# A fused attention and gated layer: the kv products' last chunk widened to 128 rows with zeros, and all lower parts of the weights made by VectorE

## The chip, the cores and the metric

One core of one Trainium2 chip runs the kernel. The metric is the time of one execution in microseconds of the device; the median of three runs is 863.46 us (861.28 to 864.54). One execution was recorded by the profiler. Engines are named as in the profile: PE is TensorE's matmuls, PEld its weight loads, DVE is VectorE, ACT ScalarE, POOL GpSimd, and SP is SyncE, which issues transfers.

## The reference

An attention without a product of queries and keys, and then a layer with two products and a gate between them.

```python
# q, k, v: (8, 8, 576, 64)
q_s = softmax(q, axis=-1); k_s = softmax(k, axis=2)      # both in the reference with exp(x - max) / (sum + 1e-9)
kv = np.einsum('bhsd,bhse->bhde', k_s, v)                # 64 x 64 for each batch and head
attn = np.einsum('bhsd,bhde->bhse', q_s, kv)
x = attn.transpose(0, 2, 1, 3).reshape(4608, 512)
h = x @ w_in                                             # 512 x 2048
g = h * np.clip(h + 3.0, 0.0, 6.0) / 6.0
out = g @ w_out                                          # 2048 x 512
```

## The kernel before

**Precision.** The weights come as 64-bit numbers, kept as pairs of 32-bit words. `decode(f)` makes fp32 values of them for one of 16 chunks `f` (128 of the 2048 columns of `w_in` and the rows of `w_out` that go with them). Each fp32 operand of a large product is split in two by `split`: ScalarE rounds it to the matmul's format (the high part), and an engine subtracts that from the value (the lower part). A product is then three matmuls: high by high, high by low, low by high.

**The decoding.** `decode(f)` works on 128 x 1024 values: ScalarE's absolute value (L133), VectorE's clamp (L134) and shift with a mask (L136), VectorE's joining of sign and exponent (L141), ScalarE's scaling of the low word (L144), VectorE's addition of it (L145), then the split (L148 to L154): ScalarE's rounding at L120 and the subtraction at L121. The subtraction of the odd chunks from 3 on is given to GpSimd by L153; these are seven: 3, 5, 7, 9, 11, 13 and 15. The others, nine, are VectorE's.

**Attention.** Heads are taken in pairs, four to a batch, so 32 pairs in all. `kv_of` makes the product of a pair's softmaxed keys and its values: 576 rows in four chunks of 128 and a fifth of 64 (`TAIL`), for each of the two heads a 64 x 65 result (the 65th column is the sum of the keys' exponentials, since the values have a column of ones). Each head writes its own half of the 128 partitions of the result `pkv`, so a matmul of a full chunk has the form 128*64 in the profile (rows*columns of the array), and one of the fifth chunk 64*64. The fp32 matmul shows as two matmuls in the trace, so a pair counts 16 and 4. `q_softmax` and `k_softmax` serve batches 0 and 1: there keys come transposed, are turned by TensorE into `pe` and `pe2`, and ScalarE copies them to `ke`, of the fifth chunk only the 64 rows that there are (L246, L247). For the later batches `token_attention` loads keys in five full chunks: the host has filled the last 64 rows of the fifth with the lowest fp32 number, whose exponential is zero, and those of the values with zeros.

**The stages.** Blocks are 512 tokens. Block 0 does attention and both products while the weights are decoded; blocks 1 and 2 do both products (`gemm1`, 12 matmuls of 512 columns into `ph`; the gate, `relu6`; the split of `g` into `gp`; `gemm2`, 12 matmuls into four `po`). The attention of a block is computed during the block before it. During block 1 VectorE also makes sums of weights (`sum_weights`), which are stored and read back. The other 3072 tokens go in three blocks of 1024 through a Strassen-like scheme of seven products instead of eight (`phase1`, `phase2`), whose weight parts are streamed from memory.

**What sets the order.** A scheduler orders the instructions of each engine by a simulation of its own. TensorE's instructions stand in the program's order only from block 1 on; in block 0 the scheduler orders them too. A change of engine for one instruction can therefore move others.

Of the kernel before, what the change touches and what calls it, by code (L numbers as in the profile page):

```python
# [10 lines left out]
F32 = mybir.dt.float32  # L11
# [7 lines left out]
P = 128  # L19
TB = 512  # L20
QD = 32
NC4 = TB // P
# [10 lines left out]
def attention_moe(  # L33
# [15 lines left out]
    nc = tc.nc  # L49

    B, NP, _, S = kT.shape
    D = q.shape[5]
# [7 lines left out]
    NCH = S // P + 1  # L60
    TAIL = S % P
# [14 lines left out]
    def bank_a(name):  # L76
        return ps_a.tile([P, TB], F32, name=name, tag="pa")
# [3 lines left out]
    def ordered(ins):  # L81
        if in_order:
            tc.keep_in_program_order(ins)

    def mm(out, lhsT, rhs, start, stop, goes_on=False):
        ordered(
            nc.tensor.matmul(  # L87
                out, lhsT, rhs, start=start, stop=stop, skip_group_check=goes_on
            )
        )  # L90

    def flip(out, in_):
        ordered(nc.tensor.transpose(out, in_, ident))
# [13 lines left out]
    def place(f, dt, name):  # L107
        return wp.tile([P, 4 * DM], dt, name=name, tag=f"w{f}")
# [7 lines left out]
    FROM_DRAM = 3  # L116
    whole = dr.tile([P, NFC, 2 * DM], F32, name="whole")

    def split(hi, lo, src, engine=nc.vector):
        nc.scalar.copy(hi, src)  # L120
        engine.tensor_sub(lo, src, hi.bitcast(F32))  # L121

    def load_w(f):
        raws[f] = place(f, U32, f"raw_{f}")
# [2 lines left out]
    def decode(f):  # L127

        n = 2 * DM
        pairs = raws.pop(f).rearrange("p (n two) -> p n two", two=2)  # L130
        low, high = pairs[:, :, 0], pairs[:, :, 1]
        m = moe.tile([P, n], F32, name="m", bufs=1)
        nc.scalar.activation(m, high.bitcast(F32), AF.Abs)  # L133
        nc.vector.tensor_scalar(m, m, W_MIN, W_MAX, op0=ALU.max, op1=ALU.min)  # L134
        m = m.bitcast(U32)
        nc.vector.tensor_scalar(  # L136
            m, m, 3, 0x3FFFFFFF, op0=ALU.logical_shift_left, op1=ALU.bitwise_and
        )
        v = moe.tile([P, n], F32, name="v", bufs=3)
        vu = v.bitcast(U32)  # L140
        nc.vector.scalar_tensor_tensor(  # L141
            vu, high, 0xC0000000, m, op0=ALU.bitwise_and, op1=ALU.bitwise_or
        )
        nc.scalar.activation(low, low, AF.Copy, scale=2.0**-29)  # L144
        nc.vector.tensor_tensor(vu, vu, low, op=ALU.add)  # L145
        if f // 2 >= FROM_DRAM:
            nc.sync.dma_start(whole[:, f], v)
        parts = place(f, F32R, f"w_{f}").rearrange("p (s i n) -> p s i n", s=2, i=2)  # L148
        split(
            parts[:, :, 0],  # L150
            parts[:, :, 1],
            v.rearrange("p (s n) -> p s n", s=2),
            nc.gpsimd if f % 2 and f > 1 else nc.vector,  # L153
        )  # L154
        wi[f], wo[f] = parts[:, 0], parts[:, 1]

# [31 lines left out]
    def kv_of(j, hp, ke, vt):  # L188
        pkv = bank_a("pkv")
        for c in range(NCH):  # L190
            r = slice(0, P if c < NC4 else TAIL)
            for h in range(2):
                hs = slice(h * D, (h + 1) * D)
                mm(pkv[hs, 0 : D + 1], ke[r, c, hs], vt[r, c, h, :], c == 0, c == NCH - 1)
        rk = att.tile([P, 1], F32, name="rk", bufs=2)
        nc.vector.tensor_scalar_add(rk, pkv[:, D : D + 1], EPS)
        nc.vector.reciprocal(rk, rk)
        kv = att.tile([P, P], F32, name="kv", bufs=10)
        nc.vector.scalar_tensor_tensor(
            kv.rearrange("p (h d) -> p h d", h=2),  # L200
            pkv[:, 0:D].rearrange("p (o d) -> p o d", o=1).broadcast_to([P, 2, D]),
            rk,
            mask.rearrange("p (h d) -> p h d", h=2),
            op0=ALU.mult,
            op1=ALU.mult,
        )
        kvs[j, hp] = kv
# [29 lines left out]
    def k_softmax(j, km, ke, kt):  # L237
        nc.vector.tensor_reduce(km, kt, axis=AX.X, op=ALU.max, negate=True)
        nc.scalar.activation(kt, kt, AF.Exp, bias=km)
        yield  # L240
        a = bank_a if j else bank
        pe, pe2 = a("pe"), a("pe2")
        for c in range(NC4):
            flip(pe[:, c * P : (c + 1) * P], kt[:, c * P : (c + 1) * P])
        flip(pe2[0:TAIL, 0:P], kt[:, TB:S])
        nc.scalar.copy(ke[:, 0:NC4].rearrange("p c n -> p (c n)"), pe)  # L246
        nc.scalar.copy(ke[0:TAIL, NC4], pe2[0:TAIL, 0:P])  # L247

    def attention(j, hp):

        if not j:
            kt, qt, qT, vt, ke = first[hp]
        else:
            kt, ke, vt = load_k(j, hp)
            qt = att.tile([P, TB], F32, name="qt", bufs=1)
            nc.sync.dma_start(qt, q[j, hp])
            qt = qt.rearrange("p (c h d) -> p c h d", c=NC4, h=2)
        km = att.tile([P, 1], F32, name="km", bufs=2)
        ks = k_softmax(j, km, ke, kt)
        next(ks)  # L260
        q_softmax(qt, j > 0, nc.vector if j else nc.gpsimd)
        yield
        next(ks, None)
        tp = (bank_a if j else bank)("tp")
        for c in range(NC4):
            flip(tp[:, c * P : (c + 1) * P], qt[:, c].rearrange("p h d -> p (h d)"))
        if j:
            qT = att.tile([P, TB], F32, name="qT")
        nc.scalar.copy(qT, tp)
        yield  # L270
        kv_of(j, hp, ke, vt)
        yield
        px = (bank_a if j else bank)("px")
        e = SHIFT * j
        for b, lo, hi in ((j - 1, 0, e), (j, e, TB)):
            if lo < hi:
                mm(px[:, lo:hi], kvs[b, hp], qT[:, lo:hi], True, True)
        x_hi, x_lo = x_block(j)
        split(x_hi[:, hp, :], x_lo[:, hp, :], px)

    def load_k(b, hp, tokens=False):
# [51 lines left out]
    def token_attention(t0, n, hp, put):  # L333
# [28 lines left out]
        for b, (ke, vt, kb) in new.items():  # L362
            kv_of(b, hp, ke, vt)
# [17 lines left out]
    def block_attention(j):  # L381
        def put(c, hp, px):
            x_hi, x_lo = x_block(j)
            split(x_hi[:, hp, :], x_lo[:, hp, :], px)

        return [token_attention(j * TB, TB, hp, put) for hp in range(NP)]
# [328 lines left out]
    for unit in units:  # L715
        next(unit)
        next(unit)
    decode(0)
    for unit in units:
        next(unit, None)  # L720
    decode(1)

    def steps(units, length):
# [32 lines left out]
    for j in range(NB):  # L756
# [10 lines left out]
        for n, f in enumerate(chunks):  # L767
            if not j and f + AHEAD < NFC:
                load_w(f + AHEAD)
            g = gemm1(j, f)  # L770
            if not j and f + 2 < NFC:
                decode(f + 2)
            if j == 1 and f % 2:
                plain_weights(f // 2, 0)
                plain_weights(f // 2, 1)
            if j:
                next(sums, None)
            for _ in range((2 if f % 4 == 3 else 1) if not j else 2 if n < 14 else 1):
                next(step, None)
            if j == NB - 1 and n == 8:  # L780
                fetch(2)
            if j == NB - 1 and n >= 14:
                for _ in range(3):
                    next(fac, None)
            pend.append((j, n, f, g))
            while len(pend) > (LAG if not j else 1):
                work(*pend.pop(0))
# [91 lines left out]
```

## Time and profile before

| what | value |
|---|---|
| median of three runs | 863.46 us (861.28 to 864.54) |
| the profiled execution, its own time | 863.42 us |
| its span from the first instruction to the last | 861.6 us |
| TensorE busy | 816.8 us (95%) |
| VectorE busy | 683.7 us (79%) |
| ScalarE busy | 443.6 us (51%) |
| GpSimd busy | 80.1 us (9%) |

The busy share of an engine is a mean over stages. In block 0, the first 146 us, VectorE is nearly always at work; later TensorE is. A row of the timeline gives start, length (both in us), engine, line, operation, output and inputs, shapes, the count of merged instructions, and in brackets how long the engine was idle before and what ended that. A row of a group gives busy time and mean length. A row of the waits gives the total in us, the times, and the longest. An instruction on VectorE is shown somewhat longer than the time after which the next one starts.

### The profile page before, as it was taken

How to read it: one execution, taken by the hardware profiler on the slowest of the kernel's cores; microseconds unless marked ns; L12 is line 12 of the kernel's file. 1: busy time of each engine (PE TensorE's matmuls, PEld its weight loads, DVE VectorE, ACT ScalarE, POOL GpSimd, SP SyncE). 2: the span in 40 equal slices, each digit the busy share in tenths (PEclk: the TensorE clock that was granted, in tenths of full speed). 3: DMA queues.
4: the chain of work that ended last, by engine and by line, in shares of the span. 5: the costliest groups of instructions: out<-in, count | busy, mean ns of one | idle time of the engine just before them, and what ended most of it. 6: DMA issues, size and time to landing. Idle time of an engine off the chain costs nothing.

```text
span 861.6 us, 11761 instructions
## 1 busy us (share of the span) xinstructions
PE 816.8 (95%) x4032; PEld 654.0 (76%) x4032; DVE 683.7 (79%) x1088; ACT 443.6 (51%) x717; POOL 80.1 (9%) x178
## 2 busy tenths in 40 slices
PE   4689998999999998999999999999999999999997
PEld 3468786877887876887877777777788788887886
DVE  7998998998778988578998985688597845648763
ACT  7886673443344444345555553544555534445543
POOL 5111212110100110001102000011000000000000
PEclk9789999999999999999999999999999999999999
DMA  9997667578549660578875667775566776666672
GB/s 366 413 407 265 210 201 233 198 243 279 169 150 366 213 240 25 169 259 272 271 256 167 194 205 238 225 229 168 172 178 193 236 231 195 193 193 191 193 234 88
DMA packets 75643, 192.30 MB, mean 223 GB/s; under 512 B 7232, under 2 KB 19520, under 8 KB 73536
## 3 DMA queue, kind: packets, MB, share of 16 engines
q1 hardware_dynamic: 75008, 190.51, 67.3%
q10 hardware_dynamic: 576, 1.05, 0.3%
q8 instruction: 32, 0.52, 0.2%
q14 instruction: 27, 0.22, 0.1%
HBM read 147.49 MB, written 44.04 MB: 222 GB/s over the span
## 4 chain that ended last, share of the span: by engine, by line
PE 67%; DVE 18%; DMA 5%; issue 4%; ACT 3%; POOL 1%; SPq 0%; ACTq 0%; DVEq 0%; POOLq 0%
PE x L87 24%; PE po L87 12%; PE ph L87 10%; PE y L87 9%; PE z L87 9%; DMA kt<-in_kT_dram 2%; DVE g L515 2%; PE px L87 2%; PE pkv L87 2%; DVE gp L121 1%; DVE gf L121 1%; DVE v L141 1%; DVE right L121 1%; DVE km L347 1%; DMA wf<-gp 1%
## 5 line engine op out<-in xcount | busy, mean ns | idle before, releaser
L120 ACT CAST gf<-g 128x512 fp32r<-128x512 f32 x168 | 103.9, 622 | 96.3 <-DVE gf L121 48.0
L87 PE MATMUL ph<-x,w 128*128 128x512 f32 x576 | 147.9, 405 | 4.4 <-POOL w L121 2.0
L87 PE MATMUL po<-w,gp 128*128 128x512 f32 x576 | 146.9, 404 | 3.5 <-DVE gp L121 2.2
L121 DVE TENSOR_TENSOR gf<-g,gf 128x512 fp32r<-128x512 f32 x168 | 112.9, 686 | 31.8 <-ACT gf L120 31.0
L87 PEld LDWEIGHTS ph<-x,w 128*128 128x128 f32 x576 | 111.7, 195 | 31.5 <-POOL w L121 2.9
L87 PEld LDWEIGHTS po<-w,gp 128*128 128x128 f32 x576 | 108.4, 192 | 29.4 <-DVE gp L121 3.3
L87 PE MATMUL x<-right,gp 128*128 128x512 f32 x384 | 95.0, 392 | 2.9 <-DVE g L555 2.9
L87 PE MATMUL x<-gf,gp 128*128 128x512 f32 x384 | 89.0, 389 | 0.0
L87 PEld LDWEIGHTS x<-right,gp 128*128 128x128 f32 x384 | 71.6, 188 | 19.2 <-DVE g L555 3.7
L87 PEld LDWEIGHTS x<-gf,gp 128*128 128x128 f32 x384 | 72.1, 188 | 15.0
L514 ACT ACTIVATE g<-ph,three 128x512 f32<-128x512 f32 x48 | 32.8, 686 | 64.6 <-PE ph L87 64.6
L120 ACT CAST gp<-g 128x512 fp32r<-128x512 f32 x48 | 29.6, 620 | 39.8 <-DVE g L515 39.7
L514 ACT ACTIVATE v<-g,three 128x1024 f32<-128x1024 f32 x24 | 27.6, 1151 | 42.4 <-DVE g L559 42.4
L87 PE MATMUL x<-right,left 128*128 128x512 f32 x192 | 47.8, 392 | 0.8 <-DVE g L555 0.8
L87 PE MATMUL y<-right,gp 128*128 128x512 f32 x192 | 48.2, 395 | 0.0
L87 PE MATMUL x<-gf,left 128*128 128x512 f32 x192 | 46.1, 392 | 0.9 <-DVE gf L121 0.9
L87 PE MATMUL z<-gf,gp 128*128 128x512 f32 x192 | 45.7, 392 | 1.0 <-DVE gf L121 0.9
L87 PEld LDWEIGHTS z<-gf,gp 128*128 128x128 f32 x192 | 35.7, 188 | 10.1 <-DVE gf L121 2.7
L87 PEld LDWEIGHTS x<-gf,left 128*128 128x128 f32 x192 | 35.7, 188 | 10.1 <-DVE gf L121 2.8
L87 PEld LDWEIGHTS x<-right,left 128*128 128x128 f32 x192 | 35.7, 188 | 8.6 <-DVE g L555 1.3
L87 PEld LDWEIGHTS y<-right,gp 128*128 128x128 f32 x192 | 35.6, 188 | 8.0 <-issue 0.5
L514 ACT ACTIVATE g<-g,three 128x512 f32<-128x512 f32 x24 | 17.4, 725 | 39.5 <-DVE g L548 39.5
(135 smaller groups left out, 1324.6 us busy)
## 6 DMA issues: line engine op xcount, KB each, us to landing
gp<-wf SPq DMA_DIRECT2D x112, 512.0 KB, 3.6
left<-wf SPq DMA_DIRECT2D x56, 512.0 KB, 3.7
raw<-in_w_dram SPq DMA_DIRECT2D x16, 1024.0 KB, 14.2
wf<-gp SPq DMA_DIRECT2D x64, 256.0 KB, 3.6
wf<-w SPq DMA_DIRECT2D x48, 256.0 KB, 3.9
vt<-in_v_dram SPq DMA_DIRECT2D x28, 325.0 KB, 5.4
kt<-in_kT_dram SPq DMA_DIRECT2D x28, 288.0 KB, 3.5
ke<-in_k_dram SPq DMA_DIRECT2D x24, 320.0 KB, 4.7
```

The source lines that it names most:

```text
L87: nc.tensor.matmul(out, lhsT, rhs, start=start, stop=stop, skip_group_check=goes_on)
L120: nc.scalar.copy(hi, src)
L121: engine.tensor_sub(lo, src, hi.bitcast(F32))
L141: nc.vector.scalar_tensor_tensor(vu, high, 0xC0000000, m, op0=ALU.bitwise_and, op1=ALU.bitwise_or)
L347: nc.vector.tensor_reduce(km, kt, axis=AX.X, op=ALU.max)
L514: nc.scalar.activation(r, h, AF.Relu, bias=three, scale=1.0)
L515: nc.vector.scalar_tensor_tensor(g, r, 6.0, h, op0=ALU.min, op1=ALU.mult)
```

## The change

Two edits. `kv_of` takes all 128 rows of every chunk, the fifth included, so that all its matmuls have the form 128*64. Where batches 0 and 1 fill `ke` from the turned keys, GpSimd now writes zeros to the 64 rows that were left unwritten: eight memsets of 64 x 128. And `split` has no choice of engine any more: all sixteen lower parts of the weights are subtracted by VectorE.

```diff
-    def split(hi, lo, src, engine=nc.vector):
+    def split(hi, lo, src):
         nc.scalar.copy(hi, src)
-        engine.tensor_sub(lo, src, hi.bitcast(F32))
+        nc.vector.tensor_sub(lo, src, hi.bitcast(F32))
...
             v.rearrange("p (s n) -> p s n", s=2),
-            nc.gpsimd if f % 2 and f > 1 else nc.vector,
         )
...
         for c in range(NCH):
-            r = slice(0, P if c < NC4 else TAIL)
             for h in range(2):
                 hs = slice(h * D, (h + 1) * D)
-                mm(pkv[hs, 0 : D + 1], ke[r, c, hs], vt[r, c, h, :], c == 0, c == NCH - 1)
+                mm(pkv[hs, 0 : D + 1], ke[:, c, hs], vt[:, c, h, :], c == 0, c == NCH - 1)
...
         nc.scalar.copy(ke[0:TAIL, NC4], pe2[0:TAIL, 0:P])
+        nc.gpsimd.memset(ke[TAIL:P, NC4], 0.0)
```

Lines behind the edits move up: by one from L154 on, by two from L191 on, and by one again from L248 on. The scheduler's order changes in blocks 0 and 1; behind these it is the same but for a few places.

At the end of block 0, VectorE's order before. `v_1160` is the last chunk's decoded weights (chunk 15, made at L145), `x1_564` is block 1's input, `g_1255` and `gp_1258` are the first gated product of block 1 and its lower part; the subtraction for chunk 15 is not among these rows, since it is GpSimd's.

```order
L145 ISA v_1160<-raw_15_942,v_1160 128x2048
L347 TENSOR_REDUCE km_1287<-kt_1281 128x1
L433 TENSOR_TENSOR v_1264<-v_1261 128x256
L435 TENSOR_TENSOR v_1264<-v_1261 128x256
L196 TENSOR_SCALAR rk_986<-pkv_975 128x1
L121 TENSOR_TENSOR gp_1153<-g_1150,gp_1153 128x512
L312 TENSOR_REDUCE qm_1291<-qt_1279 128x16
L434 TENSOR_TENSOR v_1264<-v_1264,v_1261 128x256
```

The same place after the change: `v_1168` is chunk 15's weights, `w_15_1173` their parts.

```order
L145 ISA v_1168<-raw_15_950,v_1168 128x2048
L346 TENSOR_REDUCE km_1707<-kt_1696 128x1
L432 TENSOR_TENSOR v_1272<-v_1269 128x256
L434 TENSOR_TENSOR v_1272<-v_1269 128x256
L197 SCALAR_TENSOR_TENSOR kv_997<-pkv_983,rk_994,mask_80 128x128
L304 TENSOR_TENSOR qm_1299<-qm_1299,swap_1302 128x16
L514 SCALAR_TENSOR_TENSOR g_1201<-g_1201,ph_1188 128x512
L121 TENSOR_TENSOR gp_1161<-g_1158,gp_1161 128x512
L433 TENSOR_TENSOR v_1272<-v_1272,v_1269 128x256
L121 TENSOR_TENSOR w_15_1173<-v_1168,w_15_1173 128x2x512
```

The last subtraction of the weights now stands on VectorE, nine instructions behind the last decoded chunk. Counted from the start, 198 instructions stand up to and with block 1's first lower part of g before, and 205 now.

GpSimd's order before, from its last instruction for the first attention to the first for block 2; `w_3` to `w_15` are the seven lower parts.

```order
L235 TENSOR_TENSOR kq3_109<-kq3_109,qr_166 128x512
L121 TENSOR_TENSOR w_3_422<-v_418,w_3_422 128x2x512
L121 TENSOR_TENSOR w_5_534<-v_530,w_5_534 128x2x512
L121 TENSOR_TENSOR w_7_686<-v_681,w_7_686 128x2x512
L121 TENSOR_TENSOR w_9_821<-v_816,w_9_821 128x2x512
L121 TENSOR_TENSOR w_11_972<-v_967,w_11_972 128x2x512
L121 TENSOR_TENSOR w_13_1074<-v_1069,w_13_1074 128x2x512
L349 COPY kb_1289<-km_1287 128x128
L121 TENSOR_TENSOR w_15_1165<-v_1160,w_15_1165 128x2x512
```

The same stretch now:

```order
L233 TENSOR_TENSOR kq3_109<-kq3_109,qr_166 128x512
L246 MEMSET ke_544 64x128
L246 MEMSET ke_697 64x128
L246 MEMSET ke_849 64x128
L348 COPY kb_1297<-km_1295 128x128
```

The subtractions are gone and three memsets for batch 1's keys stand in their place; the other five stand among the constants at the program's start.

TensorE's order at the start of block 0, before: `ph_339`, `ph_395` and `ph_443` are the first products of chunks 0 to 2, `pkv_473` the kv product of batch 1's first pair, `po_489` the first of the four second products.

```order
L87 MATMUL ph_339<-x0_311,w_0_306 128x512 x2
L87 MATMUL ph_395<-x0_311,w_1_334 128x512 x2
L93 MATMUL pe_425<-ident_75,kt_369 128x128 x4
L93 MATMUL pe2_426<-ident_75,kt_369 64x128
L87 MATMUL ph_443<-x0_311,w_2_366 128x512 x6
L93 MATMUL tp_434<-ident_75,qt_374 128x128 x4
L87 MATMUL pkv_473<-vt_372,ke_371 64x65 x10
L87 MATMUL po_489<-w_0_306,gp_355 128x512 x2
```

And now, with `ph_343`, `ph_399`, `ph_448` and `po_494` in the same parts:

```order
L87 MATMUL ph_343<-x0_315,w_0_310 128x512 x2
L87 MATMUL ph_399<-x0_315,w_1_338 128x512 x2
L87 MATMUL ph_448<-x0_315,w_2_370 128x512 x12
L93 MATMUL pe_429<-ident_75,kt_373 128x128 x4
L93 MATMUL pe2_430<-ident_75,kt_373 64x128
L87 MATMUL po_494<-w_0_310,gp_359 128x512 x2
```

The second products of chunk 0 now stand ahead of the turned queries and the kv product of batch 1's first pair, and behind all of chunk 2's first product.

## The prediction

> **What bounds the kernel now.** I read the page's busy shares first, then one table of busy time by stage, then TensorE's waits in block 0, then single instructions around GpSimd's subtractions and around the kv products. The stages are the start, the rest of block 0 (weights decoded while the first tokens are multiplied), the part that holds the later attention, and the rest.
>
> ```profile
> PE 816.8 (95%) x4032; PEld 654.0 (76%) x4032; DVE 683.7 (79%) x1088; ACT 443.6 (51%) x717; POOL 80.1 (9%) x178
> ...
> 0.00:40.00 40.00, 20.47 (x141) 14.59 (x142) 34.30 (x59) 31.13 (x46) 11.49 (x20) 0.87 0.97 388
> 40.00:146.00 106.00, 98.84 (x487) 78.07 (x487) 99.81 (x135) 72.87 (x147) 21.50 (x17) 0.95 0.76 272
> 146.00:620.00 474.00, 463.32 (x2381) 369.39 (x2382) 384.92 (x655) 224.25 (x346) 47.07 (x142) 0.99 0.66 213
> 620.00:861.60 241.60, 234.15 (x1027) 191.92 (x1025) 164.71 (x241) 115.34 (x180) 0.00 (x0) 1.00 0.64 194
> ```
>
> The columns behind the length of a stage are TensorE, its weight loads, VectorE, ScalarE, GpSimd, then TensorE's granted clock. From 146 us on TensorE is busy 98% of the time (463.32 of 474.00, 234.15 of 241.60) and VectorE 81% and 68%: what TensorE does there is paid in full. From 40 to 146 us it is the other way round in rank: VectorE 99.81 of 106 us (94%), TensorE 98.84 at a clock of 0.95. Both are nearly full, and who waits for whom decides.
>
> ```profile
> PE ph L87 <- POOL w L121: 2.0, 2, 1.3
> PE ph L87 <- DVE x L121: 1.3, 1, 1.3
> ...
> 105.98 4.13 PE L87 MATMUL ph<-x,w 128*128 128x512 f32 x10 [1.30 <-POOL w L121]
> ...
> 138.05 4.61 PE L87 MATMUL ph<-x,w 128*128 128x512 f32 x19 [0.72 <-POOL w L121]
> ...
> 145.89 0.74 PE L87 MATMUL ph<-x,w 128*128 128x512 f32 x2 [1.31 <-DVE x L121]
> 146.47 3.89 PE L87 MATMUL po<-w,gp 128*128 128x512 f32 x10
> ```
>
> TensorE's late waits in block 0 are for lower weight parts made by GpSimd (2.0 us) and for VectorE's lower part of x (1.3 us). So block 0 ends when VectorE and GpSimd have delivered.
>
> **The lower parts of the weights.** Seven subtractions leave GpSimd and join VectorE. What one costs there, and what it costs today:
>
> ```profile
> L121 POOL TENSOR_TENSOR w<-v,w x7: 2357/2642/2991, 39.8 to 135.2; 128x1024 fp32r<-128x1024 f32 x7
> ...
> 97.30 1.22 DVE L121 TENSOR_TENSOR w<-v,w 128x1024 fp32r<-128x1024 f32 x1
> 98.43 1.22 DVE L141 SCALAR_TENSOR_TENSOR v<-raw,m 128x1024 uint32<-128x1024 uint32 x1
> ...
> L141 DVE SCALAR_TENSOR_TENSOR v<-raw,m x15: 1210/1218/3249, 23.2 to 129.6; 128x1024 uint32<-128x1024 uint32 x15
> L136 DVE TENSOR_SCALAR m<-m x15: 679/693/2936, 22.4 to 127.8; 128x1024 uint32<-128x1024 uint32 x15
> L145 DVE CUSTOM_DVE_ANT_0 v<-raw,v x15: 1210/1216/3109, 24.6 to 132.5; 128x2048 uint16<-128x2048 uint16 x15
> ...
> 39.83 2.94 DVE L136 TENSOR_SCALAR m<-m 128x1024 uint32<-128x1024 uint32 x1
> 54.67 2.64 POOL L121 TENSOR_TENSOR w<-v,w 128x1024 fp32r<-128x1024 f32 x1 [12.46 <-ACT w L120]
> 55.14 3.25 DVE L141 SCALAR_TENSOR_TENSOR v<-raw,m 128x1024 uint32<-128x1024 uint32 x1
> 71.59 2.85 DVE L145 CUSTOM_DVE_ANT_0 v<-raw,v 128x2048 uint16<-128x2048 uint16 x1
> 91.29 3.25 DVE L141 SCALAR_TENSOR_TENSOR v<-raw,m 128x1024 uint32<-128x1024 uint32 x1
> 103.75 2.72 DVE L136 TENSOR_SCALAR m<-m 128x1024 uint32<-128x1024 uint32 x1
> 122.41 3.11 DVE L145 CUSTOM_DVE_ANT_0 v<-raw,v 128x2048 uint16<-128x2048 uint16 x1
> 134.65 0.41 DVE L435 TENSOR_TENSOR v<-v 128x256 f32<-128x256 f32 x1
> 136.71 1.57 DVE L434 TENSOR_TENSOR v<-v 128x256 f32<-128x256 f32 x1
> ```
>
> On VectorE a subtraction takes 98.43 - 97.30 = 1.13 us from its start to the next start: seven are 7.9 us more work on a nearly full engine. Against that stand seven long VectorE instructions, one inside or at the edge of each GpSimd subtraction. The one at 55.14 shows why: GpSimd's started at 54.67 and ended at 57.31, and VectorE's ended at 58.39, 1.08 us later, about its own usual length. It stood until GpSimd was through. Over the medians (L136 0.69, L141 1.22, L145 1.22; the 0.41 of L435 for L434, of the same shape) the seven lose 2.25 + 2.03 + 1.63 + 2.03 + 2.03 + 1.89 + 1.16 = 13.0 us. So the move takes 13.0 us off VectorE and puts 7.9 us on: 5.1 us less. The same rows in the order shown say that ahead of the first lower part of g in block 1 stand exactly seven more instructions than before, the subtractions, and nothing else. I take -5.1 us for the end of block 0. Bounds: at the least the 2.0 us that TensorE waits for GpSimd go; at the most TensorE's whole idle time of that stage, 106.00 - 98.84 = 7.2 us. The balance lies between, and VectorE is the engine that is late, so I keep it.
>
> The Trainium skill speaks on both sides of this. Its page "Perfetto Trace Analysis", section "Optimizing Scalar/DVE Operations", says that with a saturated VectorE handing work even to GpSimd may make sense, though between these two it might not help, as they share a read port; its page "SBUF — State Buffer", section "Who interferes with whom", says the loser of that port blocks for a whole instruction. By the first half of the former rule alone the change would cost its 7.9 us; by the latter the blocks go too. The row at 55.14 agrees with the latter.
>
> The scheduler orders block 0 anew. The first second-layer product now stands right behind the third first-layer product instead of behind the kv products too, and on SyncE two of the last raw loads stand ahead of stores of weight parts that they stood behind. Neither puts a thing that VectorE waits for further back, and VectorE's own order decides; I cost the new order at nothing, with VectorE's backlog as its cover. If that cover is gone, TensorE's idle time is what is left to win or lose.
>
> **The kv products.** One head pair now is 20 matmuls of one form instead of 16 and 4:
>
> ```profile
> 161.94 0.69 PE L87 MATMUL pkv<-vt,ke 128*64 128x65 f32 x16
> ...
> 162.10 0.40 PE L87 MATMUL pkv<-vt,ke 128*64 128x65 f32 x8
> ...
> 162.55 0.33 PE L87 MATMUL pkv<-vt,ke 64*64 64x65 f32 x4
> 162.82 0.50 PE L87 MATMUL po<-w,gp 128*128 128x512 f32 x1
> ...
> 259.24 1.83 PE L87 MATMUL pkv<-vt,ke 128*64 128x65 f32 x40
> 261.00 0.50 PE L87 MATMUL po<-w,gp 128*128 128x512 f32 x1
> ...
> 426.94 1.83 PE L87 MATMUL pkv<-vt,ke 128*64 128x65 f32 x40
> ...
> 599.30 0.95 PE L87 MATMUL pkv<-vt,ke 128*64 128x65 f32 x20
> ...
> L87 PE MATMUL pkv<-vt,ke 128*64 128x65 f32 x384 | 16.5, 228 | 0.0
> L87 PE MATMUL pkv<-vt,ke 64*64 64x65 f32 x96 | 8.0, 243 | 0.0
> ```
>
> A single group takes 162.82 - 161.94 = 0.88 us. Its 16 matmuls of the form 128*64 hold TensorE until the four of 64*64 start at 162.55: 0.61 us. Those four hold it 0.27 us. The second row is a view of the single moment 162.30: eight matmuls are under way, each 222 ns long, so one starts every 28 ns. Four more in the same run would take 0.11 us instead of 0.27: 0.16 us saved. A double group takes 261.00 - 259.24 = 1.76 us and changes form three times inside; as one run it would be 0.61 + 24 x 0.028 = 1.28 us, 0.48 saved. From 146 us to 620 there are 96/4 = 24 such groups: eight singles (first at 161.94, last at 599.30) and eight doubles (first at 259.24, last at 426.94): 8 x 0.16 + 8 x 0.48 = 5.1 us. By the last two rows, averages by form (16.5/384 = 43 ns, 8.0/96 = 83 ns), it would be 96 x 40 ns = 3.9 us. I take the middle, 4.5 us, and keep both as ends. All of it lies where TensorE is 98% busy. The eight groups ahead of 146 us save as much each, but VectorE covers them: nothing.
>
> The Trainium skill's page "TensorEngine Tiling (Array Packing)", section "Key Properties", says that a change of tiling mode drains the engine, which these rows bear out (0.27 us for four matmuls). Its section "Theoretical Speedup" speaks against the change: a contraction of 64 rows or fewer may go up to twice as fast when tiled.
>
> The zeros are eight memsets of 64 x 128 on GpSimd, two at most for one buffer's turn. The nearest row:
>
> ```profile
> 1.44 0.14 POOL L99 MEMSET mask<- 64x64 f32 x1
> ```
>
> Twice that size I call 0.2 us, 1.6 us in all, on an engine that is 9% busy, beside ScalarE's copy into the same buffer. What stands behind the last of them on GpSimd, copies of maxima for block 2's keys, is wanted only for block 2's kv products. Free; a late one would show as a kv product that waits for GpSimd.
>
> **The sum.** The profiled execution took 863.42 us (its span 861.6), next to the median 863.46. 863.4 - 5.1 - 4.5 = 853.8, rounded 854.
>
> **The rivals.** *VectorE pays and gets nothing back.* If the long instructions are long for another cause, the 7.9 us come on top of a full stage: 863.4 + 7.9 - 4.5 = 866.8, slower. For it: VectorE is at 94%. Against it: all seven fall on GpSimd's seven, and none of the fifteen medians shows it elsewhere. It decides once less than 3.4 of the 13.0 us come back. By the skill's rule of handing work to GpSimd this is the case to fear. Chance 0.04.
> *The new order starves TensorE in block 0.* Stage 40 to 146 has a clock of 0.95, so idle time there is paid again in clock (5% of 106 is 5.3 us). If the front of block 0 waits as much more as VectorE wins, only the kv term is left: 863.4 - 4.5 = 858.9, and anything up to 861. Chance 0.16.
> *The form change costs nothing by itself* and four more full matmuls replace four half ones at the same price, the case in which tiled small products are as quick as the tiling page's table hopes: 863.4 - 5.1 = 858.3. Against it: 83 ns against 43. Chance 0.07.
> *Block 1 takes the lead back.* VectorE there waits for transfers of weights that must be written and read again:
>
> ```profile
> 189.66 4.43 DMA v<-whole
> ...
> 195.61 2.86 DMA wf<-gp
> ```
>
> Both lie on the chain that ended last. If they come no earlier, the gain of block 0 stops at TensorE's slack there, and about half of 5.1 is left: 863.4 - 2.5 - 4.5 = 856.4. Chance 0.15.
>
> **How the numbers follow.** Both terms in full, 851 to 856: 0.58. The range runs from both at their best, 863.4 - 7.2 - 5.1 = 851.1, and a little below since the clock of block 0 may rise too (849.5), up to the starved case's 860.5. A measurement here tells about 0.5% (4.3 us) from no change, so faster means under 859.1: the forecast 0.58, the last two rivals 0.22, near none of the first, and a third of the starved case's 0.16 make some 0.82; I say 0.81. Slower, over 867.8, needs the first rival and more: 0.04. The rest, 0.15, is no change.
>
> **What would show it.** The first lower part of g in block 1 stands here now:
>
> ```profile
> 149.89 0.69 DVE L121 TENSOR_TENSOR gp<-g,gp 128x512 fp32r<-128x512 f32 x1 [0.69 <-ACT gp L120]
> ```
>
> Right: no VectorE row of L136, L141 or L145 over 2 us from 40 us on; TensorE's wait for GpSimd gone; this row some 5 us earlier; single kv groups near 0.72 us and doubles near 1.28, all 128*64. Wrong: VectorE's busy time from 40 to 146 us no lower in sum, new waits of TensorE for g or x in block 0, a clock below 0.95 there, or kv groups still at 0.88.

## The result, and the profile after

The changed kernel takes 852.38 us (median of six runs, 848.81 to 856.43), the kernel before beside it 862.26: a ratio of 0.9885, 95% interval 0.9854 to 0.9915. Run again in another session it took 850.45 us against 861.5, ratio 0.9856 (0.9831 to 0.988). So the change saves 10 to 11 us. The profiled execution took 852.34 us, its span 850.6.

The page's busy shares and the first three of the four stages of before (columns as there):

```profile
PE 807.8 (95%) x4032; PEld 646.5 (76%) x4032; DVE 677.9 (80%) x1095; ACT 442.6 (52%) x717; POOL 66.1 (8%) x179
...
0.00:40.00 40.00, 24.90 (x168) 18.43 (x169) 34.31 (x59) 31.93 (x46) 12.84 (x25) 0.96 0.97 390
40.00:146.00 106.00, 98.54 (x490) 75.86 (x489) 100.15 (x151) 74.75 (x152) 5.37 (x13) 0.98 0.80 283
146.00:620.00 474.00, 460.24 (x2396) 368.33 (x2395) 388.03 (x658) 226.72 (x348) 47.88 (x142) 1.00 0.64 215
```

VectorE is as full between 40 and 146 us as it was (100.15 us, before 99.81), but in that time it now does 151 instructions, before 135. Seven more instructions in the whole program, and 5.8 us less busy time (677.9, before 683.7).

The three operations that had long instances, as VectorE's groups with the shortest, median and longest length, then the first lower part of g in block 1 (the second of the two merged here, at 142.78 us):

```profile
L141 DVE SCALAR_TENSOR_TENSOR v<-raw,m x15: 1208/1219/1301, 23.1 to 124.8; 128x1024 uint32<-128x1024 uint32 x15
L136 DVE TENSOR_SCALAR m<-m x15: 678/685/695, 22.4 to 122.3; 128x1024 uint32<-128x1024 uint32 x15
L145 DVE CUSTOM_DVE_ANT_0 v<-raw,v x15: 1204/1216/1226, 24.4 to 129.1; 128x2048 uint16<-128x2048 uint16 x15
...
142.21 1.25 DVE L121 TENSOR_TENSOR gp<-g,gp 128x512 fp32r<-128x512 f32 x2
```

No instance is above 1.30 us, and block 1's first lower part stands at 142.78, 7.1 us earlier than the 149.89 of before.

TensorE's waits from 35 to 146 us (total, times, longest), all of them:

```profile
PE ph L87 <- ACT w L120: 2.6, 2, 2.3
PE po L87 <- ACT gp L120: 2.2, 3, 1.6
PE tp L93 <- DVE qt L233: 1.1, 2, 0.6
PE pe L93 <- ACT kt L237: 0.6, 1, 0.6
PE po L87 <- DVE gp L121: 0.3, 1, 0.3
PE ph L87 <- DVE w L121: 0.3, 1, 0.3
```

The wait for GpSimd's lower parts is gone, and so is that for x. TensorE now waits here mostly for ScalarE. In sum it waits as long as before in this stretch (7.1 us, before 7.2), but the stretch now holds more of its work.

The kv products, from TensorE's timeline: a single group and the product behind it, then a double one, then the two that answer to the rows at 426.94 and 599.30 of before, and the group over the whole program.

```profile
153.70 0.80 PE L87 MATMUL pkv<-vt,ke 128*64 128x65 f32 x20
154.44 0.50 PE L87 MATMUL po<-w,gp 128*128 128x512 f32 x1
...
250.44 1.39 PE L87 MATMUL pkv<-vt,ke 128*64 128x65 f32 x40
251.75 0.50 PE L87 MATMUL po<-w,gp 128*128 128x512 f32 x1
...
414.79 1.39 PE L87 MATMUL pkv<-vt,ke 128*64 128x65 f32 x40
588.50 0.80 PE L87 MATMUL pkv<-vt,ke 128*64 128x65 f32 x20
...
L87 PE MATMUL pkv<-vt,ke 128*64 128x65 f32 x560 | 20.7, 225 | 0.0
```

A single group holds TensorE for 0.74 us (before 0.88), a double one for 1.31 (before 1.76). The same four groups serve as milestones of TensorE, since they stand at the same places of the work. Ahead of them the table has the product `po` that the kernel before starts at 146.47, just behind the last wait of block 0. Each column is headed by the start in the kernel before, and the rows tell how many us earlier (negative) or later each kernel is there, in its one profile:

| kernel, its profiled span | 146.47 | 161.94 | 259.24 | 426.94 | 599.30 | 861.6 (end) |
|---|---|---|---|---|---|---|
| changed, 850.6 | -7.2 | -8.2 | -8.8 | -12.2 | -10.8 | -11.0 |
| changed, other session, 850.0 | -7.2 | -8.2 | -8.5 | -10.9 | -11.3 | -11.6 |
| weights edit alone, 856.8 | -6.3 | -7.9 | -2.9 | -4.7 | -4.7 | -4.8 |
| weights edit with the memsets, 863.3 | -3.0 | -4.6 | +1.1 | +2.0 | +1.8 | +1.7 |
| kv edit alone, 857.5 | -0.3 | -1.9 | -1.3 | -3.6 | -4.1 | -4.1 |
| GpSimd writes zeros, 852.4 | -6.9 | -8.5 | -7.9 | -10.0 | -10.3 | -9.2 |
| changed, with useless multiplications, 857.5 | +0.3 | -0.7 | -0.3 | -3.5 | -3.9 | -4.1 |

The last five rows are experiments told below. From the first column to the second four of the kernels gain 1.6 us and the other three 1.0. That is not their doing: right behind 146 us the kernel before, in its profiled execution, ran at a granted clock of 0.72. The stretch in it, and the answering one of the changed kernel:

```profile
146.00:152.00 6.00, 6.00 (x20) 4.78 (x21) 4.70 (x8) 2.70 (x5) 0.00 (x0) 0.72 0.40 131
...
139.00:145.00 6.00, 5.67 (x25) 4.38 (x24) 5.83 (x12) 4.32 (x8) 0.00 (x0) 1.00 0.20 57
```

So 7 of the 11 us are there when block 0 ends, 1 comes right behind it by this clock, and about 3 come later. Whether other executions of the kernel before slow down there too is not shown; the kernel with the fifth chunk in the middle, told below, has the same order of instructions and ran that place at 1.00.

### The profile page after: what moved, and what is told of

Read it like the earlier page. It is cut to its first block, busy times and chain, and to the rows that moved or that the text cites. A ratio compares the mean times of both kernels' runs of the same rounds, so it can differ in the third digit from the quotient of the medians.

```text
span 850.6 us, 11778 instructions
## 1 busy us (share of the span) xinstructions
PE 807.8 (95%) x4032; PEld 646.5 (76%) x4032; DVE 677.9 (80%) x1095; ACT 442.6 (52%) x717; POOL 66.1 (8%) x179
## 4 chain that ended last, share of the span: by engine, by line
PE 63%; DVE 21%; DMA 5%; ACT 4%; issue 4%; POOL 2%; SPq 0%; ACTq 0%; DVEq 0%; POOLq 0%
PE x L87 26%; PE y L87 10%; PE z L87 9%; PE po L87 8%; PE ph L87 8%; DVE gp L121 2%; DVE g L514 2%; DMA qt<-in_qf_dram 2%; PE px L87 2%; POOL swap L303 2%; DVE v L141 1%; DMA kt<-in_kT_dram 1%; DVE v L145 1%; ACT qt L219 1%; PE pkv L87 1%
## 5 line engine op out<-in xcount | busy, mean ns | idle before, releaser
L87 PE MATMUL ph<-x,w 128*128 128x512 f32 x576 | 143.8, 397 | 2.9 <-ACT w L120 2.6
L87 PEld LDWEIGHTS po<-w,gp 128*128 128x128 f32 x576 | 106.0, 189 | 33.9 <-ACT gp L120 5.9
L87 PEld LDWEIGHTS ph<-x,w 128*128 128x128 f32 x576 | 108.6, 190 | 28.4 <-ACT w L120 3.3
```

Of the source, the lines that this page charges most:

```text
L87: nc.tensor.matmul(out, lhsT, rhs, start=start, stop=stop, skip_group_check=goes_on)
```

## The experiments

**Each edit alone.** First the kernel before with the lower parts on VectorE, the kv products as they were:

```diff
-    def split(hi, lo, src, engine=nc.vector):
+    def split(hi, lo, src):
...
-        engine.tensor_sub(lo, src, hi.bitcast(F32))
+        nc.vector.tensor_sub(lo, src, hi.bitcast(F32))
...
-            nc.gpsimd if f % 2 and f > 1 else nc.vector,
```

> The kernel before with all lower parts of the weights on VectorE, the kv products as they were. Theory (GpSimd's subtractions held VectorE up, 13.0 us against 7.9 us of added work): 5 to 8 us faster, about 855 to 857 us, no L136, L141 or L145 over 2 us after 40 us, kv groups still 0.88 us. Rival (the gain of the change is the kv products', and the end of block 0 came earlier by the new order's luck): within 2 us of before.

Measured: 863.79 us against 862.07, ratio 1.0012 (0.9996 to 1.0029): nothing. Its twelve runs are not of one kind: two took 857.77 and 858.62 us, ten 862.59 to 865.47, and the profile is of the 858.62. Then the kernel before with the kv products on 128 rows and the zeros, the weights as they were:

```diff
-            r = slice(0, P if c < NC4 else TAIL)
...
-                mm(pkv[hs, 0 : D + 1], ke[r, c, hs], vt[r, c, h, :], c == 0, c == NCH - 1)
+                mm(pkv[hs, 0 : D + 1], ke[:, c, hs], vt[:, c, h, :], c == 0, c == NCH - 1)
...
+        nc.gpsimd.memset(ke[TAIL:P, NC4], 0.0)
```

> The kernel before with the kv products on 128 rows alone, GpSimd's seven subtractions kept. Theory: 24 groups behind 146 us save 0.147 us (single) or 0.442 us (double), 4.7 us in all, of which the changed kernel kept about 3: 3 to 5 us faster, 857 to 859 us, the seven long VectorE instructions still there. Rival (all of the gain is block 0's): within 1 us of before.

Measured: 857.72 us, ratio 0.9956 (0.9941 to 0.9971), so 2.5 to 5.1 us saved. Apart 0 and 4 us, together 10 to 11: the parts do not add up. The table above says where. With the weights edit alone, in the profile of the faster kind, TensorE is 7.9 us ahead at the first milestone, and 5.0 us of it are lost by the second. The largest loss is at the largest wait of TensorE in block 1, here with VectorE's rows ahead of it (the weights edit alone):

```profile
196.03 0.68 DVE L121 TENSOR_TENSOR x<-px,x 128x512 fp32r<-128x512 f32 x1
196.63 0.74 DVE L346 TENSOR_REDUCE km<-kt 128x1 f32<-128x576 f32 x1
...
198.23 0.68 DVE L311 TENSOR_REDUCE qm<-qt 128x16 f32<-128x512 f32 x1
...
209.08 0.70 DVE L321 STREAM_TRANSPOSE m<-qt 128x512 f32<-128x512 f32 x1
...
209.84 1.14 PE L87 MATMUL px<-m,kv 128*128 128x128 f32 x4 [4.02 <-DVE m L321]
```

And the same instructions in the changed kernel:

```profile
194.06 0.68 DVE L311 TENSOR_REDUCE qm<-qt 128x16 f32<-128x512 f32 x1
...
196.31 0.68 DVE L121 TENSOR_TENSOR x<-px,x 128x512 fp32r<-128x512 f32 x1
196.91 0.74 DVE L346 TENSOR_REDUCE km<-kt 128x1 f32<-128x576 f32 x1
...
204.80 0.70 DVE L321 STREAM_TRANSPOSE m<-qt 128x512 f32<-128x512 f32 x1
...
205.56 1.14 PE L87 MATMUL px<-m,kv 128*128 128x128 f32 x4 [1.10 <-DVE m L321]
```

Both kernels are at the same place at 196 us (`x<-px` and `km` stand 0.3 us apart). But the queries' maximum, L311, stands ahead of them in VectorE's queue in the changed kernel and behind them with the weights edit alone. From it to TensorE's `px` it is a chain of small steps of 11.5 us in the one (205.56 - 194.06) and 11.6 in the other. So L311 4.2 us later makes `px` 4.3 us later. That is the work of the scheduler: the kv edit, which touches neither instruction, changes its order. Over this `px` the lead on the kernel before falls from 7.3 to 4.5 us (it stands at 214.35 there, behind a wait of 1.22), and to 3.0 over the matmuls right behind it, with a granted clock of 0.89 from 200 to 215 us.

**Is it the zeros or the kv products that change the order?** The weights edit with the eight memsets, the kv products still on 64 rows.

> The first experiment's kernel (all subtractions on VectorE, fifth chunk of 64 rows) with the eight memsets added, which nothing reads; the order on TensorE and VectorE is that of the first experiment. Theory (the split's gain reaches the end of block 0 and is lost again behind it, in a wait that differs from run to run): the end of block 0 some 8 us earlier than before, then a loss in block 1 or 2; 858 to 865 us, and the profile may show the 6 us that the first profile did not. Rival (the first experiment was slow for want of the zeros, or the memsets cost time): another time than 858 or 864 us.

Measured: 864.25 us against 861.5, ratio 1.0032 (1.001 to 1.0053). The order is that of the weights edit alone, and the wait is there too (L322 here is L321 there). From TensorE's timeline and from the busy time between 215 and 290 us (granted clock third from the end), of this kernel:

```profile
213.86 1.83 PE L87 MATMUL px<-m,kv 128*128 128x128 f32 x4 [4.62 <-DVE m L322]
...
215.00:290.00 75.00, 73.11 (x375) 59.22 (x374) 54.84 (x101) 30.46 (x48) 6.40 (x28) 0.96 0.60 205
```

and of the weights edit alone in its fast profile:

```profile
215.00:290.00 75.00, 73.11 (x389) 59.73 (x388) 58.55 (x110) 31.68 (x50) 6.92 (x30) 1.00 0.62 216
```

With the same busy time of TensorE, 375 matmuls against 389 get done, at a clock of 0.96 against 1.00. So the zeros alone do not help, and the slower of these two profiles loses work to the clock behind such a wait. It does so elsewhere too: of the 6.5 us between the two spans 3.3 are there at the first column of the table already. From 50 to 55 us the granted clock was 0.66 in the slower one and 1.00 in the faster, from 103 to 109 us 0.72 and 1.00. The kernels differ by the memsets alone, and TensorE, VectorE and ScalarE have the same order in both. There is no profile of one of the ten slower runs of the weights edit alone; that they lose their time in the same way is likely, not shown, and why two of twelve escape stays open.

**Does a change of form cost, or the number of matmuls?** The kernel before with the fifth chunk in the middle of the group, so that one more change of form lies inside it and nothing else is different:

```diff
-        for c in range(NCH):
+        for n, c in enumerate((0, 1, NC4, 2, 3)):
...
-                mm(..., c == 0, c == NCH - 1)
+                mm(..., n == 0, n == NCH - 1)
```

> The kernel before with the fifth chunk of the kv products in the middle (chunks 0, 1, 4, 2, 3): the same matmuls in the same forms, but one more change of form in each group. Theory (the change of form is what costs): a single group some 0.1 us longer, 0.96 to 1.00 us instead of 0.88, the whole 2 to 4 us slower. Rival (the 64-row matmuls are slow in themselves): groups still 0.88 us and the time the same.

Measured: 863.29 us, ratio 1.0016 (1.0004 to 1.0027), so 0.3 to 2.3 us. The answering single group, from TensorE's timeline of this kernel:

```profile
162.05 1.10 PE L87 MATMUL pkv<-vt,ke 128*64 128x65 f32 x20
163.07 1.21 PE L87 MATMUL po<-w,gp 128*128 128x512 f32 x4
```

It takes 163.07 - 162.05 = 1.02 us where it took 0.88: 0.147 more by the exact starts, in the double groups too. The change takes one such step out of a single group (0.879 to 0.732) and three out of a double one (1.758 to 1.316): 0.147 each, to the last digit. Sixteen groups behind 146 us make 2.4 us; the whole is slower by 1.2 by the medians. The group is longer than the 0.96 to 1.00 us that were expected and the whole less slow than the 2 to 4 us, but the rival's 0.88 us is out. So a change of form costs 0.147 us, and four matmuls on 64 rows are no cheaper than four on 128. The Trainium skill's page "TensorEngine Tiling (Array Packing)", section "Key Properties", says that a change of tiling mode drains TensorE. These groups agree, at 0.147 us a change. The two-fold gain of its section "Theoretical Speedup" does not show. No matmul here used the other 64 rows at the same time; that this is why is argued, not shown.

**Is it GpSimd's reading that holds VectorE up?** The kernel before, with GpSimd writing zeros to its seven lower parts; the kv products unchanged:

```diff
+        if engine is nc.gpsimd:
+            nc.gpsimd.memset(lo.bitcast(F32), 0.0)
+        else:
+            engine.tensor_sub(lo, src, hi.bitcast(F32))
```

> The kernel before, but the seven lower parts that were GpSimd's are filled with zeros by it instead of subtracted: GpSimd writes as much, and reads nothing. (These lower parts are left out of the computation.) Theory A (what holds VectorE up is GpSimd's reading through a shared port): L141, L145 and the others at their usual length, 5 us or more faster. Theory B (any GpSimd work on SBUF holds VectorE up for as long as it lasts): VectorE instructions longer by the memset's length wherever they meet.

Measured: 854.2 us, ratio 0.9906 (0.989 to 0.9921): 7.9 us saved, with TensorE's form changes all still there. VectorE does not get the seven subtractions here, and its order differs from before in some 50 places. In block 1 the queries' maximum stands ahead of `x<-px` and `km`, as in the kernel before and the changed one, and the lead lasts there (-8.5, then -7.9). Lines are three further down in this kernel (L144 is the joining L141, L137 the clamp L134). A group, the memsets, and two of them with what VectorE did beside them:

```profile
L144 DVE SCALAR_TENSOR_TENSOR v<-raw,m x15: 1212/1218/1226, 23.1 to 123.4; 128x1024 uint32<-128x1024 uint32 x15
...
L122 POOL MEMSET w<- 128x1024 f32 x7 | 6.7, 956 | 88.0 <-DVE v L148 73.2 <-DMA vt<-in_v_dram 13.6 <-issue 1.2
...
50.48 0.95 POOL L122 MEMSET w<- 128x1024 f32 x1 [10.93 <-DVE v L148]
50.97 0.67 DVE L124 TENSOR_TENSOR gp<-g,gp 128x512 fp32r<-128x512 f32 x1
...
113.23 0.95 POOL L122 MEMSET w<- 128x1024 f32 x1 [14.03 <-DVE v L148]
113.30 1.42 DVE L137 TENSOR_SCALAR m<-m 128x1024 f32<-128x1024 f32 x1
```

A subtraction with two inputs ran at its usual length beside a memset (50.97 to 51.64, the memset to 51.43). The clamp, with one input and usually 0.69 us, did not: at 113.30 it took 1.42, and ended 0.54 us behind the memset. Four more clamps were stretched so, all 2.2 us together against 13.0 before. So for instructions with two inputs, 8.7 of the 13.0 us, it is the reading, as far as this run goes: no joining and no addition met a memset. For those with one, L136 with 4.3 us before and the clamp here, writing is enough; how much of their smaller loss comes from a memset's 0.95 us in place of 2.64 is not told apart. The Trainium skill's page "SBUF — State Buffer", section "Who interferes with whom", says both: that two inputs contend only with a GpSimd that reads, and that a tensor_scalar in a two-port mode contends in any case. Both agree, if the clamp is such a one (0.69 us, where a subtraction of this shape takes 1.13).

Then the other way round: the changed kernel, in which GpSimd multiplies each of the same seven chunks by one, in place, with the orders of TensorE and VectorE unchanged:

```diff
+        if f % 2 and f > 1:
+            nc.gpsimd.tensor_mul(v, v, ones.broadcast_to([P, n]))
```

> The changed kernel with seven extra GpSimd multiplications by one, in place on the same seven chunks' values: no engine's result needs them, and TensorE's and VectorE's orders stay as they are. Theory (GpSimd's reading holds VectorE up): the seven VectorE instructions of 2.5 to 3.3 us come back, VectorE is busy 10 to 14 us more ahead of 146 us, the end of block 0 comes 7 to 13 us later, 860 to 865 us. Rival (the gain came from where the subtractions stand and from their shorter latency, not from the hold-up): within 2 us of the changed kernel's 852.4.

Measured: 858.42 us against 862.47, ratio 0.9952 (0.9937 to 0.9967): 6 to 7 us of the gain are gone, which the rival cannot explain. The time is below the expected 860 to 865 us, since less of the hold-up came back: four VectorE instructions took 2.7 to 2.9 us and two more were stretched in part, 8.5 us in all instead of 10 to 14. Lines are two further down here (L143 the joining, L147 the addition). These two groups, the useless multiplications, one of them with VectorE's row in it, and block 1's first lower part (the second of two):

```profile
L143 DVE SCALAR_TENSOR_TENSOR v<-raw,m x15: 1206/1221/2915, 23.7 to 132.2; 128x1024 uint32<-128x1024 uint32 x15
L147 DVE CUSTOM_DVE_ANT_0 v<-raw,v x15: 1208/1217/2799, 25.1 to 136.5; 128x2048 uint16<-128x2048 uint16 x15
L157 POOL TENSOR_TENSOR v<-v,ones 128x1024 f32<-128x1024 f32 x7 | 20.6, 2940 | 79.3 <-DVE w L123 36.6 <-DMA whole<-v 16.8 <-DVE rk L198 13.6
...
92.89 2.24 POOL L157 TENSOR_TENSOR v<-v,ones 128x1024 f32<-128x1024 f32 x1 [4.46 <-DMA whole<-v]
93.41 2.80 DVE L147 CUSTOM_DVE_ANT_0 v<-raw,v 128x2048 uint16<-128x2048 uint16 x1
...
149.69 1.25 DVE L123 TENSOR_TENSOR gp<-g,gp 128x512 fp32r<-128x512 f32 x2
```

At 93.41 VectorE stood until GpSimd was through at 95.13 and ended 1.08 us later, just as in the kernel before. That lower part is back at 150.26, after 142.78 without the multiplications. The multiplication stands behind the chunk's split and store, so it gives nobody anything to wait for but the later owner of the buffer, and VectorE's waits up to 150 us name none for it. In the table the lead at the end of block 0 is gone (+0.3), and at the end of the program 4.1 us are left, as with the kv edit alone. So with the kv edit's order the weights edit is worth some 6 to 7 us, and there the parts do add up.

**Can the waits that are left be moved away?** In the changed kernel TensorE still waits from 380 to 520 us for VectorE (total, times, longest):

```profile
PE x L87 <- DVE g L554: 3.7, 2, 2.8
PE z L87 <- DVE gf L121: 1.7, 2, 1.2
PE px L87 <- DVE kv L197: 1.1, 2, 0.8
```

Three kernels tried to relieve VectorE there. Two issue a step of the next block's attention in every third or fourth slot of the Strassen stage in place of every second one (`if i % 2:` becomes `if i % 3 == 1:` and `if i % 4 == 1:`).

> The changed kernel with the attention of the next 1024 tokens taken up at every third slot of the first product instead of every second, so that VectorE's work for it is spread further. Theory (what was lost of the kv term between 411 and 515 us, some 2.9 us, are waits for VectorE, crowded there by that attention): TensorE's waits for VectorE at 431, 441 and 504 us shrink, 2 to 4 us faster, 848 to 851 us. Rival (VectorE has the same work in sum and the wait only moves behind): the same 852 us, with waits of like size later.

Measured: 850.27 us, ratio 0.9871 (0.985 to 0.9892), the same as the changed kernel. Its waits for VectorE from 380 to 520 us are down to one of 3.1 us for the same `g`, and no time is gained by it.

> The changed kernel with the attention of the next 1024 tokens at every fourth slot. Theory (spreading VectorE's work removes waits, and every third slot removed nearly all of them that it can): 849 to 852 us, with the 3 us wait near 436 us still there. Rival (every step of spreading brings the same again): 848 us or less.

Measured: 854.72 us, ratio 0.991 (0.9887 to 0.9933), beside it the changed kernel again:

> The changed kernel itself on the same chip, as the measure for the one beside it: 851 to 854 us; the variant at every third slot is faster if this stays above 851.5 us.

Measured: 850.45 us, as said above. Spreading further costs 4 us, and its profile has a wait of 4.1 us of TensorE's `px` for VectorE's `kv`, which was 0.8 at most in the changed kernel. The third takes work away: in `q_softmax_t` the queries' maximum is neither made nor subtracted.

> The changed kernel without the subtraction of the maximum in the softmax of the later queries (from token 1024 on): the maximum, its exchange between halves and the subtraction are left out, some 2.3 us of VectorE for each piece of 1024 tokens and head pair. Theory (between 411 and 515 us TensorE waits because VectorE's own work stands ahead of what frees TensorE's banks): TensorE's waits for VectorE between 380 and 520 us fall from 6.5 us to under 3, and 3 to 8 us are gained on the changed kernel's 850.5 to 852.4. Rival (those waits are of a chain that other work does not lengthen): the waits stay, at most 1 us is gained.

Measured: 849.84 us against 861.26, ratio 0.9862 (0.9846 to 0.9878), within 1 us of the changed kernel. Its waits in the same stretch:

```profile
PE x L87 <- ACT g L541: 2.0, 1, 2.0
PE x L87 <- DVE g L550: 1.9, 1, 1.9
PE px L87 <- DVE kv L197: 0.9, 1, 0.9
PE z L87 <- DVE gf L121: 0.5, 1, 0.5
```

Together 5.3 us, against 6.5 in the changed kernel: the wait went to another place. So these waits are not a matter of how much VectorE has to do. That they come from where single steps stand in its queue, as the one in block 1 does, is argued here, not shown. No version clearly beats the changed kernel.

## Why the prediction was right or wrong

It said 854.0 us; 852.38 and 850.45 were measured. The direction, the two mechanisms and the range held. The shares did not, and two errors partly cancel: that the sum came within 2 to 4 us is in part luck.

**Block 0, -5.1 us: the mechanism right, the size too small.** The reason given, that VectorE stands while GpSimd reads, is shown by the two kernels that take the reading away and bring it back. VectorE's own balance came out as worked out. The busy time up to block 1's first lower part (VectorE third of the engines), of the kernel before:

```profile
0.00:149.89 149.89, 123.20 (x638) 95.76 (x639) 136.94 (x197) 105.33 (x194) 32.99 (x36) 0.92 0.81 299
```

and of the changed kernel:

```profile
0.00:142.78 142.78, 120.34 (x642) 91.73 (x642) 131.39 (x205) 104.91 (x195) 18.19 (x37) 0.98 0.85 315
```

VectorE is busy 136.94 - 131.39 = 5.6 us less, 5.1 forecast. But TensorE is 7.2 us ahead at the end of block 0, the upper bound that the prediction set, and 8.2 at the first milestone. The mis-sized term is the -5.1: it counted VectorE's work alone. VectorE also waited less on its way to that row (142.78 - 131.39 = 11.39 us idle, before 12.95), and with the 5.6 that makes the 7.1 us by which the row is earlier. That this is just the bound is chance: TensorE's waits in its stage, from which it was taken, did not shrink (7.2 and 7.1 us from 35 to 146). The other 1.0 us is the clock of 0.72 behind 146 us in the profile of before. The clock ahead of 146 us rose as well, from 0.87 to 0.96 up to 40 us and from 0.95 to 0.98 behind it, but that alone does not make the lead: the kv edit alone had 1.00 and 0.97 and led by 0.3 us at the end of block 0, the weights edit alone had 0.87 up to 40 us and led by 6.3. The text named the clock only as a reason to stretch the range.

**The kv term, -4.5 us: the price right, the payment smaller.** The forecasts of 0.72 and 1.28 us are 0.732 and 1.316 in the trace, so sixteen groups save 8 x 0.147 + 8 x 0.442 = 4.7 us of TensorE. Of the changed kernel's 11.0 us only 11.0 - 8.2 = 2.8 come behind the first milestone. The table shows the lead at -12.2 and then -10.8, as TensorE meets the late steps of VectorE listed above, and runs at a clock of 0.93 from 420 to 446 us behind the longest of them (the kernel before has 1.00 from 430 to 455). The prediction's "paid in full", read from a TensorE that is 98% busy, was the loose step. Alone the edit brings 4.4 us by the medians. In its profile 0.3 us are there at the end of block 0, where VectorE was to cover everything, and does; 1.6 are the slow clock of before right behind it; 2.2 come later, so here too less than 4.7.

**The new order, costed at nothing: right for this kernel, for a reason that was not given.** The cover named was VectorE's backlog in block 0. What decided was a place in block 1, where it is worth 4.3 us whether the queries' maximum stands ahead of a few other VectorE instructions or behind them. In the changed kernel it falls well, with the weights edit alone it does not. The sum of two terms was therefore no sum of two independent things.

**The zeros, free: right.** Seven of them take 0.20 us, one 0.63, and no kv product waits for GpSimd.

**The rivals.** VectorE paying 7.9 us and getting nothing back: fell, since the blocks went. A starved TensorE in block 0: its waits there changed from GpSimd and x to ScalarE, and its lead grew; fell. The form change free by itself: fell, by the price of one change of form. Block 1 taking the lead back: it did not happen in the changed kernel (-8.2, then -8.8), but it is just what happened with the weights edit alone (-7.9, then -2.9), though through VectorE's order and not through the transfers that the rival named.

**The signs.** No long row, the wait for GpSimd gone, the earlier lower part (7 us in place of 5), the kv groups and the clock of 0.98 came as set down. One sign against the forecast came in part: TensorE's waits in block 0 for the parts of g grew from 1.0 to 2.5 us, nearly all of it for ScalarE's part, and the lead grew all the same. One sign was badly chosen: VectorE's busy time from 40 to 146 us "no lower in sum" was to speak against the forecast, and it is 100.15 us against 99.81. In a stage that an engine fills, a fixed window stays full whatever the work costs; the busy time up to the same instruction is what tells. The chances have a slip: the parts named for "faster" add up to 0.85 (0.58 + 0.22 + 0.05), not 0.82.

## What to carry to other kernels

Before handing work to an idle engine, look at the longest instance of each operation on the busy one beside its median: fifteen medians of 1.22 us with a maximum of 3.25 are a hold-up, and its sum is the price of the help. Count a lead at milestones that stand at the same work in both kernels, since an edit that wins in one stage can lose it in the next through the place of one instruction in another engine's queue. Where a scheduler sets the order, time two edits together as well as apart: here they gave 0 and 4 us apart, and 10 to 11 together. And look at the clock in the profile that serves as the measure: a slow stretch in that one execution shows as a gain of every other kernel.

## What the runs showed that was not expected

- A change of the matmul's form costs 0.147 us, the same in groups with one more, one less and three less.
- GpSimd's writing is not free for VectorE either: five clamps of 0.69 us became 0.99 to 1.42 us beside memsets of 0.95 us, while subtractions with two inputs did not.
- The hold-up has no fixed victim. In the run with useless multiplications GpSimd's own took between 2.24 us and 4.02. The first, at 43.57, took 3.95 us, and VectorE's joining beside it, at 44.54, kept its 1.22.
- One and the same program, the weights edit alone, ran in two groups of times, 858 and 863 to 865 us. The granted clock between 215 and 290 us was 1.00 in a profile of the former. In a profile of 865 us, of a program that differs by eight memsets and has the same order on the three busiest engines, it was 0.96, and 0.66 from 50 to 55 us.
